# Down projection of a linear-attention and SwiGLU block: operand roles exchanged, two additions moved into accumulating transfers, a fourth outer product split in seven

## The chip, the cores and the metric

The kernel runs on one core of a Trainium2 chip. The metric is the device time of one execution in microseconds. Engines are named as the profile names them: PE is TensorE (matmul), PEld its weight load, DVE VectorE, ACT ScalarE, POOL GpSimd, SP SyncE.

## The reference, cut to what matters

```python
x = A_x                                   # 1 x 2048 x 1024, bf16
xn = layernorm(x)
s = linear_attention(xn, wqkv, wo)        # 32 heads
h = silu(xn @ w_gate) * (xn @ w_up)       # 2048 x 3584
out = x + s * silu(h @ w_down)            # w_down: 3584 x 1024
```

Attention is the linear kind: with phi(t) = t + 1 for t > 0 and exp(t) otherwise, each head forms phi(k)'v and the sum of phi(k), and divides phi(q)(phi(k)'v) by phi(q) times that sum.

## The kernel before, in words

Every large matrix product is a two by two block product made with seven block products in place of eight (the Winograd form of Strassen's scheme). `Set` carries the accumulation in PSUM of the seven outer products 1, 5, 2, 6, 7, 3, 4 for one set of 128 rows or columns; a `Pair` runs two sets, 0 and 1, and its steps are named "product_set", so 7_1 is product 7 of set 1. An outer product can itself be split in the same way, over both sets at once: a `Joint`, in four parts named j1a to j1d for product 1. In Down a joint makes the outer product by seven inner products, each a run of seven 256-column matmuls, in place of four runs of seven 512-column matmuls; ACT moves a bank and a half to PSUM and to SBUF after part a, DVE adds in parts b and c.

The order of the steps is written out in lists: HEAD and TAIL for pairs with no joint, `LINKD` for two Down pairs that interlock (a word with "n" in front is a step of the next pair). `feed` walks them and records operations. The planner (`Plan.schedule`) then places every operation on its engine's queue by model durations and due times, and looks ahead on PE by ten operations; a DMA with later readers is held until a number of PE microseconds before it is due. Each engine runs its queue in order, and waits on semaphores are worked out from the regions that operations read and write.

Down is the last stage. h has been stored in the scratch `h_scratch` in blocks; w_down stands in SBUF as four blocks and four block combinations (`wd_load`, `wd_sum`). There are four `Group`s of 512 rows. A group loads four blocks of h of 896 KB (steps L00, L01, L11, L10) into slots of `hslots` and forms four combinations on DVE (S5, S7, S6, S3, each in slices of 1024 and 512 columns by `mk`). Group 0 has no joint; groups 1 to 3 have joints for the outer products 1, 5 and 2, for which `inner` forms four more sums each (I1, I5, I2) in the two slots of `islots`, and `inner_move` forms the matching weight sums once. The output of a block goes through `evac`: ACT's Silu into a slot of `g_ring` (from PSUM as `W<-ps`, from SBUF as `W<-TM`), a load of s into `sl_ring`, a load of x into `xo_ring`, a DVE multiplication and a DVE addition, and a store of 128 KB. All DMAs are issued by SP (helper `dma`, line 372).

Matmuls carry line 229, DVE's two-input operations line 369, ACT's line 359.

Of the kernel before, what the change touches and what calls it, by code (L numbers as in the profile page):

```python
# [14 lines left out]
KB = 1024  # L15
# [15 lines left out]
class Plan:  # L31
# [59 lines left out]
    def schedule(self):  # L91
# [29 lines left out]
        while len(order) < total:  # L121
# [37 lines left out]
            if o.sem is not None:  # L159
                free[e] = s + 0.08  # L160
# [79 lines left out]
def build_kernel(nc, A_x, A_wqkv, A_wo, B_w_gate, B_w_up, B_w_down, out, WINDOW=10, NWARM=14, NPE=4, LEAD=12.0):  # L240
# [12 lines left out]
    with ExitStack() as es:  # L253
# [120 lines left out]

        class Ring:
# [111 lines left out]
        class Set:  # L487
# [4 lines left out]
            def __init__(self, ops, evac):  # L492
                self.ops, self.evac, self.direct = ops, evac, None
# [35 lines left out]
            def sum5(self):  # L529
                self.c = balloc()  # L530
                tt([bank_r[self.b], self.s5.r], [bank_r[self.c]], ps[self.c][:, :], ps[self.b][:, :],
                   self.s5.ap(F32), ALU.add)

            def put5(self, e):
                self.s5 = s5_ring.take()
                act([bank_r[e]], [self.s5.r], self.s5.ap(F32), ps[e][:, :], ACT.Identity)
                bfree(e)

# [92 lines left out]
        LINKD = "7_0 7_1 3_0 3_1 nj1a 4_0 nj1b 4_1 nj1c nj5a nj1d nj5b nj2a nj5c nj2b nj5d n6_0 nj2c n6_1 nj2d".split()  # L631
# [4 lines left out]
        def feed(pair):  # L636

            prev = last_pair[0]
            if pair is None or not pair.joint:
                if prev is not None:  # L640
                    for w in (REST if "2" in (prev.joint or ()) else TAIL):
                        if w not in prev.did:
                            prev.do(w)
                if pair is not None:
                    for w in HEAD:
                        pair.do(w)
            else:
                third = [x is not None and "2" in (x.joint or ()) for x in (prev, pair)]
                l2 = LINKD if pair.down else LINK2
                link = LINK if not third[1] else l2 if third[0] else LINK1  # L650
                early = REST[:6] if third == [True, False] else [w[1:] for w in l2] if third[0] else ()
                for w in REST:
                    if w in early and w not in prev.did:
                        prev.do(w)
                for w in link:
                    if w[0] == "n":
                        pair.do(w[1:])
                    elif prev is not None and w not in prev.did and (w[0] != "j" or "2" in prev.joint):
                        prev.do(w)
            last_pair[0] = pair  # L660
# [428 lines left out]
        def inner_move(v, kt, at, raw=False, ms=(1, 5, 2)):  # L1089
# [3 lines left out]
            for m, places in zip(ms, at):  # L1093
# [3 lines left out]
                if raw and m != 5:  # L1097
# [21 lines left out]
        def joint_of(jstat, xin, n, s0, s1):  # L1119
# [6 lines left out]
            js = {"5": Joint(ops(5), lambda w, b: (s0, s1)[w].put5(b))}  # L1126
            if 2 in xin or n == 7:
# [109 lines left out]
        def gu_pair(p, kind, n, stats, at):  # L1237
# [15 lines left out]
            def h_done(w, i, j):  # L1253
# [4 lines left out]
                g = 2 * p + j  # L1258
                dma([s.r], [named("h", g, i, n)], h_scr[g, :, i, :, 2 * n:2 * n + 2, :].rearrange(
# [3 lines left out]
            def ev_u(w):  # L1263
                def f(i, j, ap, r, bank):
                    o, orr = part(h_slot(i, j), w)
                    act([r], [orr], o, halves(ap), ACT.Identity)
# [85 lines left out]

        def wd_load(nm, urgent):
# [10 lines left out]
        def wd_sum(o, a, b):  # L1364
            for h in range(2):
                for n0, n1 in ((0, 2), (2, 4), (4, 7)):
                    (ov, orr), (av, ar), (bv, br) = ((v[:, n0:n1], Region(r.keys[4 * n0:4 * n1]))
                                                     for v, r in (wv(nm, h) for nm in (o, a, b)))
                    tt([ar, br], [orr], ov, av, bv, ALU.subtract, True)

        DIN = {}
        DIN_AT = {(0, "1_1"): 1, (0, "5_1"): 5, (0, "2_1"): 2}
        DAT = tuple(tuple((W, (3 * m + q) * 3584) for q in range(3)) for m in range(3))
# [13 lines left out]
        hslots = Slots([(X, 0), (X, 7 * KB), (X, 14 * KB), (X, 21 * KB), (W, 38 * KB), (W, 45 * KB)], 7 * KB)  # L1387
        islots = Slots([(H, 14 * KB), (H, 21 * KB)], 7 * KB)
        R0 = 31 * KB + 512
        g_ring = Places([(W, R0), (W, R0 + KB), (W, R0 + 2 * KB)], 1 * KB)  # L1390
        sl_ring = Places([(W, R0 + 3 * KB), (W, R0 + 4 * KB), (W, R0 + 5 * KB)], 1 * KB)
        xo_ring = Places([(TM, 8 * KB), (TM, 9 * KB), (TM, 12 * KB), (TM, 13 * KB)], 1 * KB)
# [4 lines left out]
        class Group:  # L1397
# [3 lines left out]
            def __init__(self, g, cuts):  # L1401
                self.g, self.cuts, self.joint = g, cuts, g > 0
                self.s, self.j, self.done = {}, {}, set()
                self.todo = ["L00", "I1", "L01", "L11", "S5", "I5", "S7", "L10", "S6", "I2", "S3"]
                if not self.joint:
                    self.todo = [t for t in self.todo if t[0] != "I"]
                self.hold = {"00": {"S6", "S7"}, "01": {"S5", "S7", "7_1"}, "11": {"S5", "4_1"}, "10": {"S3", "3_1"},
                             "5": {"S6"}, "6": {"S3", "6_1"}}
                self.hold["00"] |= {"I1", "j1d"} if self.joint else {"1_1"}
                self.hold["5"] |= {"I5", "j5d"} if self.joint else {"5_1"}  # L1410
                self.hold["10"] |= {"I2", "j2d"} if self.joint else {"2_1"}
                if self.joint:
                    self.hold.update({"in1": {"j1d"}, "in5": {"j5d"}, "in2": {"j2d"}})

            def load(self, k, i):
                s = self.s["%d%d" % (k, i)] = hslots.take()
                for c, (n0, n1) in enumerate(self.cuts):
                    v, r = hv(s, n0, n1)
                    dma([named("h", self.g, k, n) for n in range(n0 // 2, n1 // 2)], [r], v,
                        h_scr[self.g, i, k][:, n0:n1, :], dsem("hl%d_%d" % (s.k, c)), (n1 - n0) * 64 * KB)  # L1420
# [6 lines left out]
            def try_one(self, t):  # L1427
                s, d = self.s, self.done
                if t[0] == "L":
                    if not hslots.free:  # L1430
                        return False
                    self.load(int(t[1]), int(t[2]))
                elif t[0] == "I":
                    of = {"1": "00", "5": "5", "2": "10"}[t[1]]
# [3 lines left out]
                elif t == "S5":  # L1438
                    if "01" not in s or "11" not in s or not hslots.free:
                        return False  # L1440
                    s["5"] = hslots.take()
                    self.mk(s["5"], s["01"], s["11"], ALU.add)
                elif t == "S7":
                    if "S5" not in d:
                        return False
                    self.mk(s["01"], s["00"], s["01"], ALU.subtract)
                elif t == "S6":
                    if self.joint:
                        if not {"S7", "I5", "j1d"} <= d:
                            return False  # L1450
                        s["6"] = s["00"]
                        self.hold.pop("00")
                    else:
                        if "S5" not in d or not hslots.free:
                            return False
                        s["6"] = hslots.take()
                    self.mk(s["6"], s["5"], s["00"], ALU.subtract)
                    if self.joint:
                        s.pop("00")
                elif t == "S3":  # L1460
                    if not {"S6", "j2d" if self.joint else "2_1"} <= d:
                        return False
                    self.mk(s["10"], s["10"], s["6"], ALU.subtract)
                return True

            def pump(self):
                n = 0
                while n < len(self.todo):
# [5 lines left out]
                    elif t[0] == "L":  # L1474
# [13 lines left out]
            def get(self, m):  # L1488
                return hv(self.s[{1: "00", 2: "10", 4: "11", 5: "5", 6: "6", 7: "01", 3: "10"}[m]])
# [12 lines left out]
            def dset(self, w):  # L1502
                last = self.g == 3

                def ops(m):
                    parts = []
                    for h in range(2):
                        v, r = self.get(m)
                        a, ar = v[:, 7 * h:7 * h + 7], Region(r.keys[14 * h:14 * h + 14])
                        b, br = wv(XOF[m], h)  # L1510
# [3 lines left out]
                def evac(i, j, ap, r, bank):  # L1514
                    q = g_ring.take()
                    act([r], [q.r], q.ap(FP16), ap, ACT.Silu, "ps" if bank is not None else "sb")
                    row = 512 * self.g + 256 * i + 128 * w
                    cols = slice(512 * j, 512 * j + 512)
                    t = sl_ring.take()
                    dma([named("s", self.g, w, i, j)], [t.r], t.ap(FP16), s_scr[row:row + 128, cols],  # L1520
                        dsem("sl%d" % t.k), 128 * KB).urgent = 20.0
# [5 lines left out]
                return Set(ops, evac)  # L1527
# [57 lines left out]
        for k, n in order:  # L1585
# [33 lines left out]
            if (k, n) == ("g", S_AT + 1):  # L1619
                for nm, u in (("R01", 0.0), ("R00", -15.0), ("R11", -30.0), ("R10", -45.0)):  # L1620
                    wd_load(nm, u)
                wd_sum("T1", "R01", "R00")
# [4 lines left out]
        wd_sum("T2", "R11", "T1")  # L1627
        wd_sum("T3", "T2", "R00")
        wd_sum("T4", "R10", "T2")

        def after(g, w):
# [3 lines left out]
            if (g, w) in DIN_AT:  # L1635
                m = DIN_AT[g, w]
                nm = XOF[m]
                DIN.update(inner_move({nm: (DV[nm][2], Region(DV[nm][1][0].keys + DV[nm][1][1].keys))}, NPAIR,
                                      DAT[m // 2:m // 2 + 1], True, (m,)))
        for g, c in enumerate(G):  # L1640
            words = ["%d_%d" % (m, w) for m in range(1, 8) for w in range(2)] + [
                "j%d%s" % (m, k) for m in (1, 5, 2) for k in "abcd"]
# [73 lines left out]
```

## Time and profile before

| | us |
|---|---|
| median of 3 runs | 712.01 (711.88 to 712.77) |
| profiled execution | 711.92 |
| its span | 710.2 |
| PE busy | 700.8 (99%) |
| DVE busy | 590.3 (83%) |
| ACT busy | 416.1 (59%) |
| POOL busy | 12.8 (2%) |

All times of the profile come from the profiled execution; positions are microseconds from the start of its span. Down's first matmuls stand at 540.3 us, its last ends at 705.2. The matmuls' durations are modelled and overlap, so the distance from one start to the next is what one costs.

### The profile page before, as it was taken

The numbers are of one execution on the slowest core, as the hardware profiler recorded it, in microseconds if no ns is written. First come the engines' busy times: TensorE is split into PE (matmuls) and PEld (weight loads), VectorE is DVE, ScalarE is ACT, GpSimd is POOL, SyncE is SP. The second block draws the span as 40 slices with busy tenths as digits, with TensorE's granted clock in tenths as the row PEclk, the third lists the DMA queues.
The fourth block names the chain that finished last, engine by engine and source line by source line (L and its number), as shares of the span: only waits on it lengthen the run. The fifth ranks groups of instructions, "written<-read, shape, count | busy, mean of one in ns | idle before, by whom it ended". The sixth has DMA issues, their size and how long they took to land.

```text
span 710.2 us, 11461 instructions
## 1 busy us (share of the span) xinstructions
PE 700.8 (99%) x4247; PEld 403.4 (57%) x4247; DVE 590.3 (83%) x1357; ACT 416.1 (59%) x815; POOL 12.8 (2%) x35
## 2 busy tenths in 40 slices
PE   7999999999999999999999999999999999999997
PEld 3544445555555555656566666666665466575663
DVE  5999997766998698789999876998879998676843
ACT  4767645877888886868667776675663122221211
POOL 2111000000000000000000000000000000000000
PEclk9999999999999999999999999999999999999999
DMA  9444223113211443343134126647344655446513
GB/s 300 115 90 89 52 67 119 60 60 102 77 60 64 124 119 120 119 146 92 60 118 135 56 95 222 205 152 236 120 154 136 192 175 182 141 143 216 166 35 96
DMA packets 86872, 88.96 MB, mean 125 GB/s; under 512 B 17440, under 2 KB 82720, under 8 KB 86816
## 3 DMA queue, kind: packets, MB, share of 16 engines
q1 hardware_dynamic: 86816, 88.23, 39.7%
q8 instruction: 33, 0.54, 0.3%
q14 instruction: 23, 0.19, 0.1%
HBM read 61.87 MB, written 23.20 MB: 120 GB/s over the span
## 4 chain that ended last, share of the span: by engine, by line
PE 92%; DVE 5%; DMA 1%; SPq 0%; ACT 0%; issue 0%
PE ps L229 92%; DVE H L369 2%; DMA W<-in_A_x_dram 1%; DVE W L369 1%; DVE ps L369 1%; SPq L372 0%; DVE TM L369 0%; DVE H L789 0%; PE ps L236 0%; DVE stats L701 0%; DVE stats L705 0%; ACT W L359 0%; ACT X L359 0%; DVE TM L788 0%; DVE mv L706 0%
## 5 line engine op out<-in xcount | busy, mean ns | idle before, releaser
L229 PE MATMUL ps<-P,W 128*128 128x512 f16 (+1 forms) x952 | 210.8, 341 | 0.0
L229 PE MATMUL ps<-X,W 128*128 128x512 f16 (+1 forms) x896 | 200.9, 345 | 0.0
L369 DVE TENSOR_TENSOR ps<-ps,TM 128x256 f32<-128x256 f32 (+1 forms) x292 | 145.9, 511 | 51.8 <-PE ps L229 48.5
L359 ACT ACTIVATE TM<-ps 128x512 f32<-128x512 f32 (+2 forms) x302 | 151.9, 528 | 54.8 <-PE ps L229 53.1
L359 ACT ACTIVATE H<-ps 128x512 f16<-128x512 f32 (+2 forms) x192 | 112.6, 603 | 48.2 <-PE ps L229 46.6
L229 PEld LDWEIGHTS ps<-P,W 128*128 128x128 f16 (+1 forms) x952 | 92.9, 98 | 67.3 <-issue 0.4
L229 PEld LDWEIGHTS ps<-X,W 128*128 128x128 f16 (+1 forms) x896 | 87.5, 98 | 61.7
L369 DVE TENSOR_TENSOR W<-W 128x256 f16<-128x256 f16 (+4 forms) x272 | 99.6, 402 | 19.2 <-ACT W L359 15.0
L229 PE MATMUL ps<-H,W 128*128 128x512 bf16 (+3 forms) x504 | 110.0, 355 | 0.2 <-DVE ps L369 0.2
L359 ACT ACTIVATE ps<-ps 128x256 f32<-128x256 f32 (+1 forms) x147 | 65.3, 444 | 66.1 <-PE ps L229 63.5
L369 DVE TENSOR_TENSOR H<-H 128x1024 f16<-128x1024 f16 (+6 forms) x149 | 85.8, 592 | 7.7 <-ACT H L359 6.3
L229 PE MATMUL ps<-W 128*128 128x256 f16 x504 | 88.7, 273 | 0.3 <-DVE ps L369 0.3
L369 DVE TENSOR_TENSOR TM<-ps,TM 128x512 f32<-128x512 f32 x89 | 61.1, 686 | 21.0 <-PE ps L229 20.5
L229 PE MATMUL ps<-H,X 128*128 128x512 bf16 (+3 forms) x346 | 74.2, 358 | 2.0 <-DVE nmean L718 0.8
L229 PEld LDWEIGHTS ps<-H,W 128*128 128x128 f16 x504 | 48.8, 98 | 46.9 <-DVE ps L369 0.7
L229 PEld LDWEIGHTS ps<-W 128*128 128x128 f16 (+1 forms) x504 | 49.0, 98 | 28.8 <-DVE ps L369 2.5
L229 PE MATMUL ps<-H 128*128 128x256 f16 (+4 forms) x390 | 55.0, 273 | 0.0
L229 PEld LDWEIGHTS ps<-H,X 128*128 128x128 f16 x346 | 33.2, 98 | 34.8 <-DVE H L789 1.7
L359 ACT ACTIVATE H<-TM 128x512 f16<-128x512 f32 x58 | 36.5, 630 | 12.4 <-DVE TM L369 12.3
L229 PE MATMUL ps<-W,H 128*128 128x256 f16 (+1 forms) x230 | 42.9, 317 | 0.0
L229 PEld LDWEIGHTS ps<-H 128*128 128x128 f16 (+1 forms) x390 | 34.2, 98 | 13.8 <-ACT H L359 0.3
L369 DVE TENSOR_TENSOR H<-ps,TM 128x512 f16<-128x512 f32 (+1 forms) x51 | 34.8, 685 | 5.9 <-PE ps L229 5.5
(89 smaller groups left out, 469.3 us busy)
## 6 DMA issues: line engine op xcount, KB each, us to landing
h_scratch<-H SPq DMA_DIRECT2D x56, 256.0 KB, 2.4
W<-in_B_w_gate_dram SPq DMA_DIRECT2D x7, 1024.0 KB, 5.3
W<-in_B_w_up_dram SPq DMA_DIRECT2D x7, 1024.0 KB, 5.2
H<-in_B_w_down_dram SPq DMA_DIRECT2D x4, 1792.0 KB, 7.1
X<-h_scratch SPq DMA_DIRECT2D x7, 896.0 KB, 5.2
W<-h_scratch SPq DMA_DIRECT2D x5, 896.0 KB, 4.8
W<-in_A_x_dram SPq DMA_DIRECT2D x16, 256.0 KB, 3.4
H<-in_A_wqkv_dram SPq DMA_DIRECT2D x8, 512.0 KB, 8.2
```

The lines of the kernel that those rows point to most:

```text
L229: last = h.matmul(o, l, r, start=st, stop=sp, skip_group_check=True)
L359: op = PL.op("act", reads, writes, lambda h: h.activation(o, i, func, **kw), nel(o) / 1200.0 + (0.055 if src == "ps" else 0.095))
L369: return dve(reads, writes, lambda h: h.tensor_tensor(o, a, b, op), nel(o), 1.92 if fast else 0.96)
```

## The change

- Operand roles: the block combinations of h take the part that those of w_down had, and the other way round. A group is now two half blocks of 256 rows (`row = 1024 p + 512 i + 256 h + 128 w`), h is stored in another block order, and one quarter of h and the result of product 5 change their sign (`scale=-1.0`, `sign5`).
- The sums of a group are S5, S6 and S4 on DVE. The block for product 7 is the loaded block 01 with block 11 of h added into it by a GpSimd transfer (A7, helper `dacc`): in pieces of at most 2048 columns, two for the groups 1 to 3, three for group 0. Each group then also loads block 11 itself.
- x: for groups 0 to 2 six DMAs on SP copy x into the output in the middle of the kernel (512 KB each), and each output block of 128 KB is added to it by a GpSimd transfer in place of the load of x, DVE's addition and the store. Group 3 is as before.
- Outer product 3 of groups 1 to 3 becomes a joint (`j3a` to `j3d`, I3, `put3`, `sum5` into SBUF); LINKD changes accordingly.
- Places: `hslots` has five slots in place of six, `g_ring` still three, `sl_ring` four in place of three. In the planner a DMA's issue takes its `busy` on its engine: 0.08 on SP, 1.0 on POOL.

```diff
+        def dacc(reads, writes, o, i, s, nbytes):
+            return PL.op("pool", reads, writes, lambda h: h.dma_start(o, i, accum_op=ALU.add), 1.0, sem=s, nbytes=nbytes)
...
             def sum5(self):
+                if self.third:
+                    d = self.c = s1_ring.take()
+                    tt([bank_r[self.b], self.s5.r], [d.r], d.ap(F32), ps[self.b][:, :], self.s5.ap(F32), ALU.add)
+                    return
...
+            def put3(self, b):
+                d = self.c
+                tt([bank_r[b], d.r], [d.r], d.ap(F32), ps[b][:, :], d.ap(F32), ALU.add)
+                bfree(b)
+                self.evac(0, 1, d.ap(F32), d.r, None)
...
-        LINKD = "7_0 7_1 3_0 3_1 nj1a 4_0 nj1b 4_1 nj1c nj5a nj1d nj5b nj2a nj5c nj2b nj5d n6_0 nj2c n6_1 nj2d".split()
+        LINKD = ("7_0 j3a 3_0 7_1 j3b 3_1 j3c 4_0 j3d nj1a 4_1 nj1b nj5a nj1c nj5b nj1d nj5c nj2a nj5d nj2b nj2c nj2d n6_0 n6_1"
+                 ).split()
+        RESTD = "7_0 j3a 7_1 j3b 4_0 j3c j3d 4_1".split()
...
-        DIN_AT = {(0, "1_1"): 1, (0, "5_1"): 5, (0, "2_1"): 2}
+        DIN_AT = {(0, "1_1"): 1, (0, "5_1"): 5, (0, "2_1"): 2, (0, "3_1"): 3}
...
-        hslots = Slots([(X, 0), (X, 7 * KB), (X, 14 * KB), (X, 21 * KB), (W, 38 * KB), (W, 45 * KB)], 7 * KB)
+        hslots = Slots([(X, 0), (X, 7 * KB), (X, 14 * KB), (X, 21 * KB), (W, 42 * KB)], 7 * KB)
...
+        g_ring = Places([(W, o * KB) for o in (49, 50, 51)], 1 * KB)
+        sl_ring = Places([(TM, o * KB) for o in (8, 9, 12, 13)], 1 * KB)
+        xo_ring = Places([(W, o * KB) for o in range(8)], 1 * KB)
...
-                self.todo = ["L00", "I1", "L01", "L11", "S5", "I5", "S7", "L10", "S6", "I2", "S3"]
+                self.todo = ["L00", "I1", "L01", "S5", "I5", "L10", "I2", "A7", "S6", "S4", "L11", "I3"]
...
+            def accumulate(self, nm, k, i):
+                s = self.s[nm]
+                for c, (n0, n1) in enumerate(self.cuts):
+                    for q, (a0, a1) in enumerate(((n0, n0 + 8), (n0 + 8, n1)) if n1 - n0 > 8 else ((n0, n1),)):
+                        v, r = hv(s, a0, a1)
+                        rd, a = self.src(k, i, a0, a1)
+                        dacc(rd + [r], [r], v, a, dsem("ha%d_%d" % (s.k, 2 * c + q)), (a1 - a0) * 64 * KB)
...
+                    tt([q.r, t.r], [q.r], q.ap(FP16), q.ap(FP16), t.ap(FP16), ALU.mult, True)
+                    if self.g < 3:
+                        dacc([q.r, named("ox", self.g, i)], [named("oo", row, j)], of[row:row + 128, cols], q.ap(FP16),
+                             dsem("oa%d" % q.k), 128 * KB)
+                        return
                     x = xo_ring.take()
                     dma([], [x.r], x.ap(), xf[row:row + 128, cols], dsem("xo%d" % x.k), 128 * KB).urgent = 20.0
-                    tt([q.r, t.r], [q.r], q.ap(FP16), q.ap(FP16), t.ap(FP16), ALU.mult, True)
                     tt([q.r, x.r], [x.r], x.ap(), q.ap(FP16), x.ap(), ALU.add, True)
                     dma([x.r], [], of[row:row + 128, cols], x.ap(), dsem("oo%d" % x.k), 128 * KB)
...
+        for g in range(3):
+            for i in range(2):
+                row = 1024 * (g // 2) + 512 * i + 256 * (g % 2)
+                dma([], [named("ox", g, i)], of[row:row + 256, :], xf[row:row + 256, :], dsem("ox%d%d" % (g, i)),
+                    512 * KB).urgent = 250.0
```

More of the change, by code (lines that the diff above doesn't have):

```diff
@@ L159, in schedule @@
             if o.sem is not None:
[L160 removed]
+                free[e] = s + o.busy
                 t0, rate, t1 = self.ALONE if o.start < self.RUSH else self.MIXED
@@ L640, in feed @@
                 if prev is not None:
-                    for w in (REST if "2" in (prev.joint or ()) else TAIL):
+                    for w in RESTD if prev.down else REST if "2" in (prev.joint or ()) else TAIL:
                         if w not in prev.did:
@@ L657, in feed @@
                         pair.do(w[1:])
-                    elif prev is not None and w not in prev.did and (w[0] != "j" or "2" in prev.joint):
+                    elif prev is not None and w not in prev.did and (w[w[0] == "j"] in (prev.joint or ())) == (w[0] == "j"):
                         prev.do(w)
@@ L1431, in try_one @@
                         return False
-                    self.load(int(t[1]), int(t[2]))
+                    self.load(t[1:], int(t[1]), int(t[2]))
+                elif t == "S5":
+                    if "01" not in s or not hslots.free:
+                        return False
+                    s["5"], s["7"] = hslots.take(), s.pop("01")
+                    self.mk(s["5"], s["00"], s["7"], ALU.add)
+                elif t == "A7":
+                    self.accumulate("7", 1, 1)
                 elif t[0] == "I":
-                    of = {"1": "00", "5": "5", "2": "10"}[t[1]]
+                    of = {"1": "00", "5": "5", "2": "10", "3": "11"}[t[1]]
                     if of not in s or not islots.free:
```

122 lines of the change are left out of this document (52 added, 70 removed).

## The prediction

> **What bounds the kernel now.** I read the page's busy shares and its chain first, then the waits of TensorE, then busy time by stretch, and last the matmuls of the last stage in order of time.
>
> ```profile
> span 710.2 us, 11461 instructions
> PE 700.8 (99%) x4247; PEld 403.4 (57%) x4247; DVE 590.3 (83%) x1357; ACT 416.1 (59%) x815; POOL 12.8 (2%) x35
> q1 hardware_dynamic: 86816, 88.23, 39.7%
> PE 92%; DVE 5%; DMA 1%; SPq 0%; ACT 0%; issue 0%
> PE ps L229 <- DVE ps L369: 0.3, 1, 0.3
> core 0: us, PE busy (x) PEld busy (x) DVE busy (x) ACT busy (x) POOL busy (x), PEclk, DMA share, GB/s
> 333.80:355.40 21.60, 21.29 (x134) 12.54 (x132) 21.56 (x53) 15.87 (x33) 0.00 (x0) 1.00 0.15 50
> 540.30:569.20 28.90, 28.90 (x135) 13.13 (x134) 28.69 (x47) 5.35 (x9) 0.00 (x0) 1.00 0.45 140
> 540.30:705.20 164.90, 164.87 (x982) 95.90 (x980) 123.64 (x234) 36.22 (x68) 0.00 (x0) 1.00 0.45 146
> ```
>
> TensorE is the bound. The fifth line is all that the matmuls waited for between 60 and 705 us: 0.3 us. The last row is the Down stage: 164.87 of 164.90 us are matmuls, at full granted clock. DVE has 41 us free there over the whole stage, though 0.2 us in its first 29 us. POOL does nothing after the first stages, and the one queue with data is SP's: **no row of this trace shows a transfer that GpSimd issues, or one that adds**. The span is 710.2 us, the profiled execution 711.92 us, so 1.7 us lie around the span; the median of the three runs is 712.01. I make the sum against 711.92. A change of 0.2%, 1.4 us, is about what a measurement of this kernel can tell from none.
>
> **What it saves on TensorE.**
>
> ```profile
> 567.73 1.67 PE L229 MATMUL ps<-P,X 128*128 128x512 f16 x7
> 569.24 0.93 PE L229 MATMUL ps<-H,X 128*128 128x256 bf16 x7
> 570.00 1.67 PE L229 MATMUL ps<-H,W 128*128 128x512 bf16 x7
> 571.51 0.93 PE L229 MATMUL ps<-H 128*128 128x256 f16 x7
> ```
>
> From start to start a run of seven 512-column matmuls takes 569.24 - 567.73 = 1.51 us, one of seven 256-column matmuls 0.76 us (570.00 - 569.24). Outer product 3 of a group is two sets of two such runs, 4 x 1.51 = 6.04 us. As seven inner products it is 7 x 0.76 = 5.35 us (0.764 before rounding). That is 0.70 us a group, and three groups have it: **-2.1 us**, all on the bound. Exchanging the operand roles, by itself, leaves count and shape of the other matmuls, so I give it nothing.
>
> **DVE and ACT, in the same stage.**
>
> ```profile
> L369 DVE TENSOR_TENSOR X<-X 128x1024 f16<-128x1024 f16 x22 | 14.5, 682 | 0.0
> L369 DVE TENSOR_TENSOR TM<-W,TM 128x512 bf16<-128x512 f16 x31 | 12.6, 418 | 0.3
> L369 DVE TENSOR_TENSOR TM<-ps,TM 128x512 f32<-128x512 f32 x14 | 9.7, 690 | 7.6 <-PE ps L229 7.6
> L369 DVE TENSOR_TENSOR ps<-ps,TM 128x256 f32<-128x256 f32 x18 | 7.7, 430 | 11.9 <-PE ps L229 11.4
> L369 DVE TENSOR_TENSOR H<-X 128x896 f16<-128x896 f16 x10 | 5.9, 617 | 0.0
> L369 DVE TENSOR_TENSOR W<-H 128x1792 f16<-128x1792 f16 x2 | 2.2, 1082 | 0.0
> L369 DVE TENSOR_TENSOR X<-X 128x512 f16<-128x512 f16 x8 | 3.3, 416 | 0.0
> L359 ACT ACTIVATE W<-TM 128x512 f16<-128x512 f32 x14 | 8.8, 630 | 48.0 <-DVE TM L369 48.0
> L359 ACT ACTIVATE ps<-ps 128x256 f32<-128x256 f32 x9 | 3.3, 368 | 9.7 <-PE ps L229 9.7
> ```
>
> Gone: one of four h sums a group, 3 x 0.68 + 0.42 = 2.46 us, four times, and 24 x additions of 0.42: 19.8 us. Added in each of three groups: four inner sums of 0.62, two additions of 0.69 and two of 0.43, 4.7 us; and once four weight sums of 1.08: 18.4 us. Nothing on balance, on an engine with 41 us free. The weight sums follow product 3 of group 0, so after the stretch where DVE is full. ACT gains some 2 us of moves at 36 of 165. All this lies beside the matmuls.
>
> **SP and the early stages.** SP loses 24 loads of x and 24 stores of the output, keeps the four h loads of a group, and gains six copies of x straight into the output, 512 KB each, placed in the middle of the kernel at a time of low DMA share. Nobody near them needs their data. But the schedule written out by the planner shifts from there on, and the order of matmuls differs through the stretch at 334 to 355 us, where DVE is busy 21.56 of 21.60 us and TensorE idles 0.31 (rows above). I take 0; the bound is 1 us lost (three such gaps) or 0.3 gained.
>
> **The accumulating transfers** are the open term. POOL gets 9 adds into an h slot (896 KB a group, in pieces of 512 and 384) and 24 adds of 128 KB into the output, all on one queue in order. Each of the 24 holds one of only three slots of `g_ring` until it has landed; before, a slot came free after DVE's addition. The nearest rows:
>
> ```profile
> X<-h_scratch SPq DMA_DIRECT2D x7, 896.0 KB, 5.2
> TM<-in_A_x_dram SPq DMA_DIRECT2D x32, 128.0 KB, 2.6
> out_dram<-TM SPq DMA_DIRECT2D x32, 128.0 KB, 2.3
> 583.77 0.43 SPq L372 DMA_DIRECT2D TM<-in_A_x_dram  x1
> 593.71 0.32 SPq L372 DMA_DIRECT2D X<-h_scratch  x1
> 705.21 0.60 ACT L359 ACTIVATE W<-ps 128x512 f16<-128x512 f32 x1 [0.91 <-DVE TM L369]
> 706.30 0.42 DVE L369 TENSOR_TENSOR TM<-W,TM 128x512 bf16<-128x512 f16 x1
> ```
>
> From 128 to 896 KB a landing grows by 2.6 us, so a plain transfer costs 3.4 ns a KB and about 2.2 us besides. The lower end for an add is that price. The upper end is a load and a store one after the other, which is what the adds replace: twice the bytes' time, 6.8 ns a KB. I take the upper end, since an add must read both operands and so moves the load's bytes and the store's. The Trainium skill says so too: "Collectives: The Full Stack" (The bandwidth ceiling: the fold count and why AG ≠ RS ≠ AR) states that an add inside a DMA engine is slow for its two source reads, not for the adding, and gives a measured ratio of 1.93; no run here shows it so far. For POOL's issue I take the schedule's own 1.0 us; SP's is 0.32 to 0.43.
>
> Now the crossing from group 1 to group 2, time 0 at the end of product 7's second set, in the program's order. DVE makes the first half of sum 5, then POOL issues the 512 KB add at +1.95 (matmul end, one TM addition, two sums), then the output add of 7 (128 KB), the 384 KB add, and the output add of 3's first set (128 KB, its product ready at +6.7, since four inner sums stand ahead of it on DVE). ACT is in order: the Silu of 3's second set takes 7's slot, and the Silu of 4's second set takes that of 3's first. Behind them stand ACT's moves of the joint products 1 and 5 of the next group, on which TensorE waits.
> - First: TensorE needs the moves at +10.6 (j3b's last run, j3c, 4_0, j3d, j1a, 4_1 lie between); less 0.74 for two moves and 0.63 for the Silu, 7's slot must be free at +9.2. It is free at 1.95 + 1.0 + 2.2 + d, with d for 640 KB: 2.2 plain, 4.35 doubled, so at +7.3 or +9.5: stall 0 or 0.3.
> - Second: j5b comes at +16.0, so the slot must be free at +14.6. Data start at about +4.0; 512 + 128 + 384 + 128 = 1152 KB cost 3.9 plain, 7.8 doubled; about 1 us to land; the next group's h load of 896 KB (3.0) and part of another (1.0) share the DMA engines. Free at +12.9 or +16.8: stall 0 or 2.2.
>
> So 2.5 us at that crossing when adds cost double, none when plain. Group 2 to 3 has the same pattern, and there DVE also stands in order at sum 6, waiting for the 384 KB piece with joint 5's additions behind it: I take 2.5 there. Group 0 to 1 has its 3s early and wide: I take 0.7. Together **+5.7 us**.
>
> The tail stays: the last product is still 4's second set, in group 3 with the old loads, Silu 0.60, two DVE steps of 0.42 and a store.
>
> Sum: 711.9 - 2.1 + 0 + 5.7 = **715.5 us**, slower by 0.5%.
>
> A page's rate beside that of the rows: the two landings above differ by 2.6 us for 768 KB. The Trainium skill, "DMA: Bandwidth & Descriptors" (Anatomy of one DMA — SWDGE (gpsimd) path), gives for GpSimd's transfers about 2.0 us and the bytes at 436 GB/s, which would be 1.8 us for the same 768 KB; doubled, the 1152 KB of the second deadline would then take 5.4 us, and by that estimate the sum would be 709.8 us, the time of the first rival.
>
> **The rivals.**
> - *Adds at a copy's price, no stall* (the other side). Place: the three slots at the crossings. By the lines above the second deadline holds until the 1152 KB take 14.6 - 4.0 - 1 - 4 = 5.6 us, 1.4 times plain. Below that the matmul saving comes out whole: 709.8; with the 1 us of the early stages 710.8. For it: the rate of 128 KB loads has room, DMA share in Down is 0.45. Against: both operands must be read.
> - *Adds far slower than two passes*, four times plain: the slack is gone already at two, so each crossing loses another 1152 KB x 6.8 ns = 7.8 us, 23.5 in all: 739; at three times, 727. For it: nothing shows how fast the adding unit runs, and the output adds also change type. Against: none.
> - *The early stages pay*: adds nearly plain, but the shifted order at 334 to 355 us loses 1 us and the crossings another 0.7: 711.5. For it: DVE full there; against: the idle of 0.31.
>
> **How the numbers follow.** Forecast (two passes) 0.42; its own range, with issue and fixed time up to 1 us off on either side of each deadline, 712.5 to 722, all but its edge slower. Adds at a copy's price 0.30, of which 0.22 faster by over 0.2% and 0.08 within it. Far slower adds 0.18. Early stages 0.10: 0.08 within, 0.02 slower. So faster 0.22, within 0.16, slower 0.62. The range reaches down to the copy's price, 709.8, and up to some three passes, 729; above it lie about 0.13, below 0.06.
>
> **What would show it.** Right: in Down, ACT's W<-ps and W<-TM Silus wait for a DMA into out_dram, then TensorE for ACT or DVE near j1b and j5b, with gaps of 0.3 to 3 us at two crossings, and the adds land in some 5 us (128 KB, alone) to 10 (384 KB). Matmul runs of the stage sum to 162.8 us plus gaps. Wrong: no TensorE gap in Down (then 710), landings of 15 us and more (then 727 and up), or gaps before 540 us.

## The result, and the profile after

| | before | after |
|---|---|---|
| median | 712.06 us (711.73 to 712.83, 20 runs) | 713.38 us (712.80 to 714.86, 20 runs) |
| profiled execution | 711.92 us | 713.16 us |
| its span | 710.2 us | 711.2 us |

The ratio is 1.002 (95% interval 1.0013 to 1.0027): slower, by 1.3 us where 3.5 was forecast. The profiled executions differ by 1.24 us.

The page of the kernel after (busy times; queues with packets, MB and the share of 16 engines; the chain):

```profile
span 711.2 us, 11606 instructions
PE 699.2 (98%) x4310; PEld 408.4 (57%) x4310; DVE 588.7 (83%) x1345; ACT 417.3 (59%) x821; POOL 41.5 (6%) x68
q1 hardware_dynamic: 80096, 85.08, 38.4%
q0 software_dynamic: 4752, 6.82, 6.1%
PE 91%; DVE 3%; DMA 3%; SPq 1%; issue 0%; ACT 0%; POOL 0%; POOLq 0%
```

q0 is the new queue of GpSimd's transfers. DMA on the chain went from 1% to 3%.

Where TensorE stood still in Down, by its waits from 540 to 706 us (us in total, times, longest):

```profile
PE ps L229 <- DVE ps L369: 1.5, 2, 0.9
```

and by the matmuls around the two places, in order of time (start, us):

```profile
673.02 0.93 PE L229 MATMUL ps<-H 128*128 128x256 f16 x7
674.86 0.94 PE L229 MATMUL ps<-W,H 128*128 128x256 f16 x7 [0.91 <-DVE ps L369]
...
676.39 0.93 PE L229 MATMUL ps<-W,H 128*128 128x256 f16 x7
677.93 0.94 PE L229 MATMUL ps<-W,X 128*128 128x256 f16 x7 [0.60 <-DVE ps L369]
```

A run of seven should follow the one before it by 0.76 us. 674.86 - 673.02 = 1.84 and 677.93 - 676.39 = 1.54: 1.08 and 0.77 us lost, 1.85 in all, both at the crossing from group 2 to group 3. There is no other gap in Down.

In the early stages the waits of TensorE and of its weight loads (330 to 380 us) are, in the kernel after:

```profile
PEld ps L229 <- DVE H L369: 1.2, 3, 0.6
PEld ps L229 <- DVE ps L369: 1.0, 4, 0.3
...
PEld ps L229 <- DVE TM L369: 0.7, 2, 0.5
...
PE ps L229 <- DVE H L369: 0.3, 1, 0.3
PE ps L229 <- DVE TM L369: 0.2, 1, 0.2
```

and in the kernel before (its 0.3 us of TensorE stands in the prediction):

```profile
PEld ps L229 <- DVE ps L369: 1.3, 4, 0.6
...
PEld ps L229 <- DVE H L369: 0.4, 2, 0.2
```

From the starts of the matmuls in that stage, less the usual distance of their shapes, 1.41 us are lost after and 0.47 before: +0.93.

The tail: DVE's last addition in the kernel after, in order of time (the kernel before's is the last row of the prediction's transfers, 706.30):

```profile
core 0 of [0], span 711.2 us
...
706.53 0.42 DVE L369 TENSOR_TENSOR W<-W 128x512 bf16<-128x512 f16 x1
```

From its start to the end of the span are 710.2 - 706.30 = 3.9 us before and 711.2 - 706.53 = 4.7 after. The last store lands 3.65 us after the last matmul starts in both traces; what runs on are SP's closing waits, one for every semaphore that a transfer used, 0.06 us for two of them: to 5.02 us after the last matmul's start before, to 5.75 after.

The account of the profiled executions, in us:

| | forecast | found |
|---|---|---|
| matmul work of the split | -2.1 | -2.08 |
| early stages | 0 | +0.93 |
| crossings 0 to 1, 1 to 2, 2 to 3 | +0.7, +2.5, +2.5 | 0, 0, +1.85 |
| tail | 0 | +0.7 |
| outside the span | 0 | +0.24 |
| first 30 us (loads) | 0 | -0.5 |

The rows add up to 1.1 of the 1.24 us; what is missing is rounding. The last row is chance: by the starts of the matmuls, the profiles below, whose first stages are the same, differ there by up to 1.7 us. Effects under a microsecond are therefore read from the stage, not from the time alone.

### The profile page after: what moved, and what is told of

Its sections match the earlier page's. It is cut to its first block, busy times and chain, and to the rows that moved or that the text cites. A ratio compares the mean times of both kernels' runs of the same rounds, so it can differ in the third digit from the quotient of the medians.

```text
span 711.2 us, 11606 instructions
## 1 busy us (share of the span) xinstructions
PE 699.2 (98%) x4310; PEld 408.4 (57%) x4310; DVE 588.7 (83%) x1345; ACT 417.3 (59%) x821; POOL 41.5 (6%) x68
## 3 DMA queue, kind: packets, MB, share of 16 engines
q0 software_dynamic: 4752, 6.82, 6.1%
## 4 chain that ended last, share of the span: by engine, by line
PE 91%; DVE 3%; DMA 3%; SPq 1%; issue 0%; ACT 0%; POOL 0%; POOLq 0%
PE ps L229 91%; DMA X<-h_scratch 2%; SPq L372 1%; DVE H L369 1%; DMA W<-in_A_x_dram 1%; DVE W L369 1%; DVE ps L369 0%; DVE H L803 0%; DVE stats L715 0%; DVE stats L719 0%; ACT H L359 0%; ACT TM L359 0%; DVE TM L369 0%; ACT W L359 0%; POOL out_dram L376 0%
## 5 line engine op out<-in xcount | busy, mean ns | idle before, releaser
L229 PE MATMUL ps<-P,W 128*128 128x512 f16 (+1 forms) x896 | 196.6, 339 | 0.3 <-DVE H L369 0.3
L229 PEld LDWEIGHTS ps<-P,W 128*128 128x128 f16 (+1 forms) x896 | 87.4, 98 | 62.1 <-DVE H L369 0.6
L369 DVE TENSOR_TENSOR TM<-ps,TM 128x512 f32<-128x512 f32 x101 | 69.3, 687 | 26.4 <-PE ps L229 25.9
L229 PE MATMUL ps<-H,W 128*128 128x512 f16 (+3 forms) x406 | 88.9, 353 | 0.2 <-DVE ps L369 0.2
L369 DVE TENSOR_TENSOR W<-W 128x256 f16<-128x256 bf16 (+4 forms) x240 | 85.1, 392 | 3.8 <-PE ps L229 3.5
L229 PE MATMUL ps<-H,X 128*128 128x512 bf16 (+3 forms) x402 | 80.1, 346 | 1.7 <-DVE nmean L732 0.7
L229 PEld LDWEIGHTS ps<-H,W 128*128 128x128 f16 x406 | 39.2, 98 | 36.5 <-DVE ps L369 0.7
L229 PE MATMUL ps<-P,X 128*128 128x512 f16 x224 | 51.9, 379 | 0.0
L229 PE MATMUL ps<-W,H 128*128 128x256 f16 (+1 forms) x272 | 48.5, 310 | 1.1 <-DVE ps L369 0.9
L229 PEld LDWEIGHTS ps<-H 128*128 128x128 f16 (+1 forms) x432 | 38.2, 98 | 15.7 <-ACT H L359 0.3
L359 ACT ACTIVATE W<-TM 128x512 f16<-128x512 f32 x20 | 12.6, 630 | 56.0 <-DVE TM L369 50.8
```

The lines of the kernel that those rows point to most:

```text
L229: last = h.matmul(o, l, r, start=st, stop=sp, skip_group_check=True)
L359: op = PL.op("act", reads, writes, lambda h: h.activation(o, i, func, **kw), nel(o) / 1200.0 + (0.055 if src == "ps" else 0.095))
L369: return dve(reads, writes, lambda h: h.tensor_tensor(o, a, b, op), nel(o), 1.92 if fast else 0.96)
```

## The experiments

**Two waits at the end.** SP's closing waits cut to the stores and adds into the output, in the kernel after (e1) and in the kernel before (e2):

```diff
-        for s in semn.values():
-            if id(s) in PL.count:
+        for nm, s in semn.items():
+            if id(s) in PL.count and nm[:2] in ("oo", "oa"):
```

> The kernel after, with SP's closing waits only for the semaphores of the transfers that write the output (out_dram from W, from X and from TM), not for every semaphore of every transfer. Accounting of the two traces: the closing waits are a serial list of about 0.06 us for two semaphores, and end 5.75 us after the last matmul starts while the last store lands at 3.65; before's end at 5.02. If that list ends the kernel, 1.5 to 2.1 us go: 711.4 (711.2 to 712.0). Rival, the end is set by the landing of the last store and a fixed close: no change, 713.4 (within 0.3).

> The kernel before with the same cut of SP's closing waits (only those for the transfers into the output). If the list of waits ends the kernel, 0.8 to 1.4 us go: 710.9 (710.6 to 711.3), less than in the kernel after, whose list has some 24 more semaphores; the change alone then costs 0.5 us, not 1.3. Rival, the end is set by the last store: 712.06 as before.

Measured: 711.54 us (ratio to the kernel before, on the same chip, 0.999, 0.9981 to 0.9999), and 710.82 (0.9985, 0.9976 to 0.9994; the kernel before 712.34). The span and DVE's last addition of e1, and of e2:

```profile
core 0 of [0], span 710.2 us
...
707.58 0.43 DVE L369 TENSOR_TENSOR W<-W 128x512 bf16<-128x512 f16 x1
```

```profile
core 0 of [0], span 708.7 us
...
706.09 0.42 DVE L369 TENSOR_TENSOR TM<-W,TM 128x512 bf16<-128x512 f16 x1
```

Both tails are now 2.6 us, and the difference of 0.8 is gone: the list of waits ended both kernels, and the change had made it longer.

**The copies of x.**

```diff
-                    512 * KB).urgent = 250.0
+                    512 * KB).urgent = 400.0
```

> The kernel after, its six copies of x into the output given an earlier due time (urgent 400 in place of 250), so that the planner places them before the stage at 320 to 375 us and not in it; nothing else is changed. Theory, the copies made the planner order that stage's matmuls differently and that order costs 0.93 us: the gaps of PE at 332 to 375 us go, 712.4 (712.2 to 712.8). Rival, the 0.93 us are the reordered projection of Down's weights (the sums of R01, R11) or the copies' own traffic wherever they lie: 713.4 within 0.3.

Measured: 712.53 us (ratio 1.0005, 0.9995 to 1.0014). TensorE waits for nothing from 300 to 540 us, and what is left of the weight loads' waits for DVE is:

```profile
PEld ps L229 <- DVE H L369: 0.3, 1, 0.3
PEld ps L229 <- DVE ps L369: 0.3, 1, 0.3
```

By the starts of the matmuls the stage loses 0.20 us, against 1.41; Down's 1.86 stay. So where the planner put the copies had reordered the matmuls of the busiest stage, and that order cost the 0.93. It is not the copies' own traffic: in the kernel after the last of the six lands at 316.2 us, ahead of the stage, and in e7 below, where four of them run between 303.7 and 314.0 us but the order is another, the stage loses 0.30.

**Copies in place of adds.**

```diff
-            ... h.dma_start(o, i, accum_op=ALU.add), 1.0, ...
+            ... h.dma_start(o, i), 1.0, ...
```

> The kernel after with the same GpSimd transfers at the same places in every queue, but as plain copies: the sum of h11 and h01 and the addition of x to three quarters of the output are left out. Theory, an adding transfer takes its engines twice as long per byte as a copy, and the stall at the crossing from group 2 to group 3 (0.9 and 0.6 us beside each other, 1.86 in all) is the 384 KB piece of the h sum landing late: the share of the software queue falls from 38% to near 20%, the 384 KB pieces land in 5 to 6.5 us in place of 9.4, the two gaps at 675 and 678 us go, 711.6 (711.3 to 712.1). Rival, the late landing is the GpSimd queue (issues of 0.85 us one behind another, waits in its order) whatever the transfer does: the gaps stay and so does the time, 713.4 within 0.4.

Measured: 712.05 us (ratio 1.0003, 0.9994 to 1.0012). The queue's row and the 384 KB pieces, then the same of the kernel after (the queue's stands above):

```profile
q0 software_dynamic: 4400, 6.82, 3.3%
X<-h_scratch POOLq DMA_DIRECT2D x3, 384.0 KB, 4.5
```

```profile
X<-h_scratch POOLq DMA_DIRECT2D x3, 384.0 KB, 9.4
```

For the same 6.82 MB the engines take 3.3% of the span as copies and 6.1% as adds, 1.85 times. No wait of TensorE is left in Down. So it is the adding that made the stall, and not the order of GpSimd's queue, which is the same here; the time lies at the upper edge of what was expected. One thing e4 does not separate: an issue also holds GpSimd shorter, 0.54 us in place of 0.85.

**Which adds.** Only the h transfers as copies (e5), only the output transfers as copies (e6):

```diff
# e5
-                        dacc(rd + [r], [r], v, a, ...)
+                        dacc(rd + [r], [r], v, a, ..., plain=True)
# e6
-                        dacc([q.r, named("ox", self.g, i)], ...)
+                        dacc([q.r, named("ox", self.g, i)], ..., plain=True)
```

> The kernel after with the h transfers as plain copies and the output transfers still adding (the sum of h11 and h01 is left out); every queue keeps its order. Reading of the trace: at the crossing from group 2 to 3 the 512 and 384 KB adds move 896 KB at about 5.5 ns a KB, 2.3 us more than copies would, and two things wait for them: ACT's Silu for the output add queued behind the 512 KB piece, and sum 6 for the 384 KB piece itself. So without their second source the two gaps at 675 and 678 us (1.85 together) shrink to under 0.3. Rival, the slots of g_ring and the output adds' own price set the gaps: at least 1.2 us stays.

> The other half: output transfers as plain copies (x is not added in three quarters of the output), the h transfers still adding. Reading of the trace: only 3 x 128 KB of the traffic ahead of the 384 KB piece gets cheaper, by some 4 ns a KB, 1 to 1.5 us; the 384 KB piece lands in 10 to 11 us in place of 11.8, and the gaps go from 1.85 to 0.4 to 1.1. Rival, the slots and the output adds' own price set the gaps: under 0.3.

Measured: 712.23 us (1.0001, 0.9992 to 1.0011) and 712.96 (1.0016, 1.0005 to 1.0026). e5 has no gap in Down. e6 has two, 1.10 and 0.30 us by starts, 1.40 in all, more than I expected: its 384 KB piece still lands in 11.4 us against 11.8. The waits of e6:

```profile
PE ps L229 <- DVE ps L369: 0.9, 1, 0.9
DVE X L369 <- DMA X<-h_scratch: 0.9, 1, 0.9
```

The h adds make the stall; the output adds lengthen it by some 0.4 us.

**Four slots.**

```diff
-        g_ring = Places([(W, o * KB) for o in (49, 50, 51)], 1 * KB)
-        sl_ring = Places([(TM, o * KB) for o in (8, 9, 12, 13)], 1 * KB)
+        g_ring = Places([(W, o * KB) for o in (49, 50, 51)] + [(TM, 13 * KB)], 1 * KB)
+        sl_ring = Places([(TM, o * KB) for o in (8, 9, 12)], 1 * KB)
```

> The kernel after with four places in g_ring (one is taken from sl_ring), so that a Silu waits for the output add four blocks earlier, not three. The planner makes the order anew, the early stages too, so Down alone is read. Theory, the wait that ends last at the crossing from group 2 to 3 is sum 6 for the 384 KB piece: ACT's waits for transfers into the output fall from 9.5 us to under 4, but TensorE's gaps there stay at 1.2 to 2.2 us. Rival (the step of the prediction that put the slots first): the gaps fall below 0.7 with them.

Measured: 714.02 us (1.0027, 1.0014 to 1.0039). In Down ACT waits for no transfer into the output any more, 9.5 us in the kernel after, and yet DVE and then TensorE wait (the waits, and the order of time):

```profile
DVE X L369 <- DMA X<-h_scratch: 3.4, 1, 3.4
```

```profile
678.52 1.65 PE L229 MATMUL ps<-W,X 128*128 128x256 f16 x7 [2.03 <-DVE ps L369]
```

Freed from the slots, DVE reaches sum 6 earlier and waits there longer; the 384 KB piece itself, now behind three output adds and not two, lands at 677.07 us, 0.9 later than in the kernel after. The slots alone don't end that crossing. The gap lies at the upper end of my 1.2 to 2.2, 2.2 us by starts, and about 1.7 more are lost behind it, of which below.

**The planner's price, the loads later.**

```diff
# e8
-                dma_free = b + o.nbytes / rate
+                dma_free = b + (2 * o.nbytes if e == "pool" else o.nbytes) / rate
# e9
-   ....urgent = 20.0 if self.g else 50.0
+   ....urgent = 0.0 if self.g == 3 else 20.0 if self.g else 50.0
```

> The kernel after, the planner charging a GpSimd transfer twice its bytes (in dma_free only), which the trace shows an add to cost. Nothing of the work changes, only the order. Theory, the stall of Down is one of order: two loads of 896 KB for group 3 are placed 2 to 7 us after product 7's end, on the same engines as the adds; with the true price the planner moves loads and adds apart, and the gaps at the crossing from 2 to 3 fall below 0.4; the early stages keep their 0.9, so 711.6 (711.2 to 712.2). Rival, the doubled traffic finds no place at any crossing: the gaps move to another crossing and 713 stays.

> The kernel after, the due times of group 3's h loads brought 20 us later (urgent 0 for that group alone); the planner then orders the end of Down anew. Theory, the crossing from 2 to 3 stalls because two loads of 896 KB share the engines with the adds 2 to 7 us after product 7 there (4 us earlier than at the crossing from 1 to 2): with the loads later the gaps at 665 to 680 us fall from 1.85 to under 0.6, if the loads then come early enough for group 3's own sums. Rival, the adds alone are too late or the traffic is too much wherever it lies: 1.2 us or more stays, there or at another crossing.

Measured: e8 715.90 us (1.0045, 1.0031 to 1.006), its profiled run 713.65; e9 712.64 (1.0002, 0.9993 to 1.0011). In e8 the gap did not go, it only moved, to an earlier place of the same crossing:

```profile
666.75 0.63 ACT L359 ACTIVATE W<-TM 128x512 f16<-128x512 f32 x1 [3.77 <-DMA out_dram<-W]
...
668.01 0.94 PE L229 MATMUL ps<-W,H 128*128 128x256 f16 x7 [1.63 <-ACT TM L359]
```

Here it is a slot of `g_ring` that comes late, as the prediction had put it for the crossing from 1 to 2. In e9 one gap of 0.61 us by starts is left, at the edge of what was expected:

```profile
674.71 0.94 PE L229 MATMUL ps<-W,H 128*128 128x256 f16 x7 [0.45 <-DVE ps L369]
```

Of the two loads only the second moved: it comes 7.3 us after the 512 KB add (668.17 and 660.84 us) and not 5.0, while the first still comes 0.5 us after it. With that most of the stall goes, though e9 also orders the end of Down otherwise, so the loads' share is not proved by it alone.

**DVE makes the h sum.**

```diff
-   self.todo = [..., "I2", "A7", "S6", "S4", "L11", "I3"]
+   self.todo = [..., "I2", "L11", "A7", "S6", "S4", "I3"]
...
-                    self.accumulate("7", 1, 1)
+                    if "11" not in s:
+                        return False
+                    self.mk(s["7"], s["7"], s["11"], ALU.add)
```

> The kernel after with the sum of h01 and h11 made by DVE (block 11 is loaded once, ahead of it, and DVE adds in slices: 2.5 us a group) in place of the adding GpSimd transfers; the output adds stay. Theory, the h adds are what stalls the crossing from 2 to 3, and DVE has the room: TensorE's gaps there fall to under 0.5 us, POOL issues 24 transfers in place of 33, and the rest stays, so 711.5 (711.0 to 712.4). Rival, DVE has no room at the crossings, or the slots of g_ring then wait as long: gaps of 1 us and more, 712.5 to 714.

Measured: 712.48 us (1.0005, 0.9996 to 1.0015), its profiled run 711.77. One gap of 0.62 us by starts is left, behind ACT's waits for slots; gap and time both lie a little above what I expected:

```profile
ACT W L359 <- DMA out_dram<-W: 7.3, 4, 3.4
```

```profile
668.66 0.94 PE L229 MATMUL ps<-W,H 128*128 128x256 f16 x7 [0.45 <-DVE ps L369]
```

**All together**: the h sum on DVE, four slots, the short closing waits (the edits above).

> What the runs point to, together: DVE's h sum, four places in g_ring, and closing waits only for transfers into the output. From the kernel after's accounts: -1.85 in Down, -0.9 in the early stages (the order that four places gave showed none of it), -1.5 for the closing waits: 713.2 less 4.2, 709.0 (708.5 to 710.0), faster than the kernel before by 0.4% and than the kernel before with the same closing waits (710.8) by some 0.25%. Rival: a wait takes the place of those removed, 710.5 or more.

Measured: 709.28 us (708.50 to 709.81), ratio 0.9959 (0.9947 to 0.9972). It beats the kernel before and, by 1.5 us, the kernel before with the short closing waits, though those two were not timed side by side, nor on the same chip. Its waits in Down:

```profile
core 0 of [0], span 707.6 us
...
ACT TM L359 <- DMA out_dram<-TM: 2.5, 1, 2.5
```

TensorE itself waits for nothing from 300 us to the end of Down.

**The split taken out**: no joint for product 3, the adds as in the kernel after.

```diff
-            if n == 7:
-                js["3"] = Joint(ops(3), lambda w, b: (s0, s1)[w].put3(b))
...
-        RESTD = "7_0 j3a 7_1 j3b 4_0 j3c j3d 4_1".split()
+        RESTD = "7_0 3_0 7_1 3_1 4_0 4_1".split()
```

> A part alone: the kernel after with its accumulating transfers, exchanged roles and places, but outer product 3 of the groups 1 to 3 left as two sets of outer products (no I3, no inner weight block 3). Theory, splitting product 3 is worth 0.70 us a group on TensorE: its matmul runs in Down cost 2.1 us more from start to start, and since product 3's Silus no longer stand between the moves the stall at the crossing from 2 to 3 may shrink from 1.85 to between 0 and 1.5; together 713.2 to 715.2. Rival, the split's four extra inner sums and additions cost on DVE what it saves on TensorE: 712.5 or less.

Measured: 713.72 us (1.0021, 1.0012 to 1.003). TensorE waits for nothing in Down, though ACT waits longer than ever for the output:

```profile
ACT W L359 <- DMA out_dram<-W: 9.9, 5, 4.3
```

Within the intervals the kernel after is no faster with the split than without: the split's 2.1 us were given back as 1.85 of stall. In the order without it no gap shows, so there the adds had time enough.

**What a stall costs beyond its length.** Three kernels were profiled again, unchanged: e8 twice (e13, e14), e7 (e15), and the kernel after (e16).

> The kernel of e8_planner_price unchanged, for another profile. Its profiled run (713.65) had one gap of 1.6 us after 664 us and full clock behind it; its other four took 715.5 to 716.2. Theory, in those runs the gap was longer (2 us or more) and TensorE's granted clock fell to about a half for some 3.4 us behind it, which costs 1.7 us: a profile of such a run shows the clock below 0.7 at 668 to 672 us and 715.5 to 716.2. Rival, the 2 us come from the start of the kernel or from outside the span: full clock after 664 us whatever the time.

> The same kernel and the same question as the run beside it: a time near 715.9 goes with a clock below 0.7 behind the gap, a time near 713.7 with full clock (rival: no such pairing).

> The kernel of e7_ring4 unchanged, whose times spread from 711.6 to 716.5 and whose profiled run (714.78) had a gap of 2.0 us with granted clock 0.57 in the 4 us behind it. Theory: where the gap is under 2 us the clock holds and the time is 712.5 to 713.5; where it is longer the clock halves and the time is 714 or more. Rival: gap and clock do not go together.

> The kernel after, unchanged, beside the others on this chip. Theory: its two gaps of 1.1 and 0.8 us are too short to cost the clock, which stays at 1.00 behind them; 712.8 to 713.9 with Down's gaps at 1.5 to 2.0 in all. Rival: the clock falls behind its gaps too, 714 or more.

Measured, one time each: 714.54, 712.89, 714.43 and 713.59 us. By the starts, e13's gap is 1.85 us, e14's 1.73, e16's two 0.95 and 0.74, with the clock at 1.00 in the 4 us behind each. e15's is 2.4. Stretches behind the gap (their columns are those of the table by stretch in the prediction), of e7, then of e15:

```profile
678.50:682.50 4.00, 3.98 (x18) 2.58 (x19) 0.80 (x2) 0.60 (x1) 0.00 (x0) 0.57 0.00 0
```

```profile
678.10:682.10 4.00, 3.95 (x19) 2.29 (x20) 1.87 (x4) 0.60 (x1) 0.00 (x0) 0.66 0.00 0
```

So in Down the clock fell behind gaps of 2.2 and 2.4 us and not behind gaps up to 1.85. The other half of that theory missed: e13 took 0.9 us more than e8's profiled run with the clock at 1.00 behind its gap, and 0.8 of it lies in the first 30 us. There the clock did fall: it was 0.50 from 11.15 to 14.56 us, after TensorE had stood still for 0.47 and 1.41 us. Why four of e8's five timed runs took 715.5 to 716.2 stays open; none of its three profiles shows such a run.

## Why the prediction was right in direction and wrong in size

**Right: the saving.** -2.1 forecast, -2.08 found, on the bound.

**Right: an add costs nearly two passes.** It takes the engines 1.85 times a copy's time (e4). The Trainium skill's ratio of 1.93 for two source reads ("Collectives: The Full Stack", The bandwidth ceiling: the fold count and why AG ≠ RS ≠ AR) agrees with that within 4%. Adds at a copy's price and adds far slower, two of the rivals, fall.

**The step that failed: the time at which the second slot comes free at the crossing from 1 to 2.** The forecast added it up from a price per KB and fixed times: +16.8, a stall of 2.2 us. It came at +14.2, and there is no stall. The deadlines were worked out from the order and the issue times, and these came out: product 7's second set ends at 615.38 (time 0), the 512 KB add is issued at +2.1 (forecast 1.95), the output add of 3's first set at +6.9 (forecast 6.7).

```profile
613.71 1.67 PE L229 MATMUL ps<-P,X 128*128 128x512 f16 x7
...
617.50 0.85 POOL L376 DMA_DIRECT2D X<-h_scratch  x1 [3.08 <-DVE X L369]
...
618.04 1.20 POOL L376 DMA_DIRECT2D out_dram<-W  x1
...
618.77 1.35 POOL L376 DMA_DIRECT2D X<-h_scratch  x1
...
622.25 0.86 POOL L376 DMA_DIRECT2D out_dram<-W  x1 [2.12 <-DVE W L369]
...
623.74 0.63 ACT L359 ACTIVATE W<-TM 128x512 f16<-128x512 f32 x1 [2.41 <-DMA out_dram<-W]
...
629.60 0.60 ACT L359 ACTIVATE W<-ps 128x512 f16<-128x512 f32 x1 [4.40 <-DMA out_dram<-W]
```

Both Silus wait for slots, as forecast, until +8.4 (forecast 9.5, deadline 9.2) and +14.2 (forecast 16.8, deadline 14.6). Each is inside its deadline, the second by 0.4 us, so TensorE does not stop. The two queues over the stretch from 617.4 to 627 us, 9.6 us long:

```profile
q0 software_dynamic: 437, 1.05, 61.4%
q1 hardware_dynamic: 291, 1.03, 28.8%
```

61.4% of 9.6 us is 5.9 us for 1.05 MB: 5.75 ns a KB, where I had put 6.8. SP's transfers paid 2.75 and not 3.4. By its packets the whole step's data ran from 619.1 to 629.1 us, so 10.0 us where 7.8 + 4.0 = 11.8 were forecast. In that time the adds' 1152 KB took 6.7 us of the engines' time in place of 7.8; SP moved more than I had reckoned, 1.47 MB, in the 4.0 us of the forecast; and the two overlapped by 0.7. The start of the data (+3.7 for +4.0) and the landing (0.4 us behind the last data for 1.0) gave the rest of the 2.6 us by which the slot came early. So the price alone does not account for it: with 6.7 us for the adds and my other terms as they were, the slot would have come at +15.7, 1.1 us too late.

The price is no constant either. By the same reckoning over the whole span (the queues' rows of the page above) the adds cost 6.5 ns a KB and SP's transfers 3.3, close to what I had put; two output adds with little beside them (633 to 637 us) cost 9.3. My price was one number for every size and place, the difference of two median landings, and it was too high for this stretch. Beside it: the rate that the Trainium skill gives ("DMA: Bandwidth & Descriptors", Anatomy of one DMA — SWDGE (gpsimd) path), 436 GB/s, is by my estimate 2.35 ns a KB and 4.7 when doubled, as far below the 5.75 as my 6.8 lay above it, and its 709.8 left no stall at all and came out too low.

**2 to 3 is not "the same pattern".** Forecast 2.5, found 1.85. The waits are those named, slot and sum 6 (e8 and e10 show the slot alone, e7 sum 6 alone). But from the slot to TensorE the way is another: the first gap runs through DVE, whose multiplication waits for the late Silu (671.63) and stands ahead of three sums and of the addition that TensorE needs, and not through ACT's moves. And the traffic is another: the next group's loads come 0.5 and 5.0 us after the 512 KB add, at 1 to 2 they come 4.0 and 8.5 after it. SP's issues of 896 KB at 1 to 2 (the add stands above, 617.50), then the add, SP's issues, the late Silu with DVE's multiplication behind it, and sum 6 at 2 to 3:

```profile
621.49 0.32 SPq L372 DMA_DIRECT2D X<-h_scratch  x1
...
626.04 0.32 SPq L372 DMA_DIRECT2D W<-h_scratch  x1
...
660.52 0.85 POOL L376 DMA_DIRECT2D X<-h_scratch  x1 [0.65 <-PE ps L229]
...
661.02 0.32 SPq L372 DMA_DIRECT2D W<-h_scratch  x1
...
665.57 0.32 SPq L372 DMA_DIRECT2D X<-h_scratch  x1
...
671.63 0.63 ACT L359 ACTIVATE W<-TM 128x512 f16<-128x512 f32 x1 [1.57 <-DMA out_dram<-W]
672.29 0.42 DVE L369 TENSOR_TENSOR W<-W,TM 128x512 f16<-128x512 f16 x1 [1.63 <-ACT W L359]
...
676.16 1.03 DVE L369 TENSOR_TENSOR X<-X 128x1024 f16<-128x1024 f16 x2 [1.36 <-DMA X<-h_scratch]
```

The 512 and 384 KB adds land in 8.4 and 11.8 us here, in 5.4 and 7.3 there. The 0.7 at 0 to 1, for which no row spoke, was not found.

**Taken at nothing and not nothing.** The early stages: +0.93, inside the bound of 1 us that I gave and put at 0; e3 and e7 show it to be the order and not the traffic. The tail: I followed the last store to its landing and did not follow SP's queue to its end; the closing waits are queued behind that store, and the change's new semaphores lengthened them (e1, e2). With the order mended alone the change stands at 1.0005 of the kernel before (e3); with the closing waits cut on both sides 0.7 us are left between the two (711.54 and 710.82).

So the mechanism was right at one of three crossings, and errors on both sides hid each other: 3.85 us of stalls too many, 1.9 us of small costs too few. The direction was luck, too: the stall that was found, 1.85, is less than the 2.08 saved, so by the forecast's own terms the change would have come out even or a little faster. What made it slower are the costs that I had put at nothing. (One slip in the sums: DVE's additions that go come to 19.9 us and not 19.8; nothing hangs on it.)

## What to carry to other kernels

An accumulating transfer occupied the DMA engines 1.85 times as long as a copy, so what it needs is a gap in the other traffic: lay the loads that are due soon against it before counting deadlines, and take the price from the queue's share of the engines in a stretch like the one in question, since here it ran from 5.75 to 9.3 ns a KB. When parts of a sum are put at nothing, add up their bounds: here they decided the direction. Follow every queue to its last instruction, waits included: here the waits that close the kernel before cost it 1.3 us by its trace and 1.5 by the medians, not far from the 2.1 us of matmuls that the change saved. When an edit elsewhere lets a planner shift the order in a stage that is full, put the edit where the order stays.

## What was not expected of the hardware

TensorE's granted clock fell to 0.57 and 0.66 in the 4 us behind gaps of 2.2 and 2.4 us, and cost some 1.7 us more than the gap; behind Down's gaps of 1.85 us and less it stayed at 1.00. The Trainium skill, "TensorE: Matmul & The Clock Gate" (Part 1: The HAM clock gate), has the clock halve after at least one idle window of about 3.4 us; here gaps shorter than that window were enough.

It need not be one gap, either. In these traces the clock changes in steps of 3.41 us: it was 0.50 from 678.58 to 681.99 us in e7, from 679.38 to 682.79 in e15, and from 11.15 to 14.56 in e13, each time for one step. If such steps are laid through all 18 profiles from the clock's first rise on, every step that was followed by a fall had TensorE idle for 1.87 us or more in total (e13's 1.87, in two gaps; e7's 2.03; e15's 2.19), and every step that was not had 1.87 or less (e13's gap in Down 1.69, e8's 1.60). The ends of the matmuls are modelled, so the limit is rough. It would mean that the place of a gap in the step counts as well as its length.

An adding transfer also holds GpSimd longer, 0.85 us an issue against 0.54 as a copy.
